# Leftover rows in the tiling of their neighbour, logits beside v, and a first tile over two queues

## The chip, the cores and the metric

One core of one Trainium2 chip. The metric is the device time of one execution in microseconds, the slowest (here the only) core. The kernel before takes 213.19 us (median of 3 runs, 213.16 to 213.43). The span in a profile is about 1.7 us shorter than the device time of the same run (211.4 against 213.11).

Engines are named as in the profile: PE is the matrix engine, PEld its weight loads, DVE VectorE, ACT ScalarE, POOL GpSimd, SP the queue engine that issues most DMAs.

## The reference

The input is x, 2048 x 512. It is layer-normalised, and two branches of it are added to x:

```
xn  = layernorm(x)
# A: 32 heads of 16, a dilated window of 8 keys (distance 0, 2, .. 14)
q, k, v = split(xn @ wqkv);  a = softmax(q.k over the window / 4);  A = (sum a v) @ wo
# B: gated MLP with spatial mixing, F = 1376, Fh = 688
z   = gelu(xn @ w_in);  z1 = z[:, :688];  z2 = layernorm(z[:, 688:])
g   = w_sp @ z2 + b_sp[:, None]           # w_sp is 2048 x 2048
B   = (z1 * g) @ w_out                    # w_out is 688 x 512
out = x + A + B
```

688 = 5 x 128 + 48: the last product contracts over five full chunks and 48 leftover rows. `g` for one tile of 128 rows is called a spatial product below; there are 16.

## The kernel before

All parts are cut. Tensors of 512 columns are handled in four blocks `tb` of 512 rows, each of four tiles; `o` counts output blocks of four tiles.

The matrix engine is used in several tilings. A full pass contracts over 128 rows into 128 columns. `wo` is applied in four row tiles of 32 (K=32, four passes into four PSUM banks run together), the leftover rows of `w_out` in two row tiles of 64 (K=48), logits and v in four column tiles of 32.

```python
def v_mm(d2):                                   # column tiling (0, 32*tb)
    for dd in range(2):
        for kc in range(C):
            for tb in range(TB):
                PE.matmul(pv[32*tb:32*tb+32, dd, :], wv[:, kc, 2*d2+dd, :], xnT[...],
                          ..., tile_position=(0, 32 * tb))
    A.copy(vp[:, 2*d2:2*d2+2, ...], pv[:])

def out_mm(o, last=False):
    for d in range(DH):                         # wo: row tiling, K=32, four at once
        for tb in range(TB):
            PE.matmul(pos[tb], op[32*tb:32*tb+32, d, ...], wo_r[32*tb:32*tb+32, d, :],
                      ..., tile_position=(32 * tb, 0))
    for h in range(2):
        pair = (2 * h, 2 * h + 1)
        for tb in pair:                         # leftovers: K=48, two at once
            r = slice(64 * (tb % 2), 64 * (tb % 2) + FH - FULL)
            PE.matmul(pos[tb], uT[r, o % 2, MCH-1, ...], wout[r, MCH-1, :],
                      ..., tile_position=(64 * (tb % 2), 0))
        for tb in pair:                         # five full passes each
            for m in range(MCH - 1):
                PE.matmul(pos[tb], uT[:, o % 2, m, ...], wout[:, m, :], ...)
        # ... add x, store
```

```python
load_x0(SP, 0); load_x0(A, 2); load_x0(SP, 1); load_x0(A, 3)   # four tiles of x, 128 KB each
load_wqk(SP, 0)                       # first half of the q and k weights, 512 KB
SP.dma_start(xall[:, 1], xblk[1])     # block 1 of x, 512 KB
load_wqk(SP, 1)                       # second half
# ... blocks 2 and 3 of x, then w_z2

warm_up(9)                            # nine passes on zeros, for PE's clock
# ... layer norm of tile 0, transposes, warm_up(2), tile 1, then the q and k products
```

```python
# order of the middle part (cut)
logits(3); prods(5); sm_max(0)
z2s(1, 1)
v_mm(0)
z2s(1, 2)
logits(4); ...
z2s(1, 3)
v_mm(1)
z2s(2, 0)
logits(5); ...
PE.transpose(pb[:], b16[:], ident[0:NT, 0:NT]);  A.copy(b_col[:], pb[:])   # b_sp to columns
...
z2_stat_act(2, 3)                     # 1/sqrt of z2's variance: root on ACT, reciprocal on DVE

for n in range(16):                   # one spatial product each
    z1_mm(n); gs = g_mm(n)
    # 2 to 5 DVE steps of softmax(..) * v ("applies")
    u_mul(n, gs)                      # z1 * g on DVE, then a DMA transpose into uT
    if n % 4 == 3 and o > 0: out_mm(o - 1); load_xr(o)
out_mm(3, last=True)
```

## Time and profile before

| what | value | view |
|---|---|---|
| span | 211.4 us | page |
| PE busy | 204.3 us, 97% | page, busy table |
| DVE, ACT busy | 83%, 45% | page, busy table |
| PE in one unbroken chain | from 24.2 to 207.8 us | chain of waits |
| PE idle that the list of waits finds, without its last line | 2.9 us | waits of PE |
| one output block | 8.74 us | chain in order of time |

The page's line of busy times, one engine after the other with its share of the span and its instructions:

```profile
PE 204.3 (97%) x1712; PEld 120.1 (57%) x1716; DVE 174.8 (83%) x248; ACT 95.2 (45%) x151; POOL 3.9 (2%) x20
```

The list of waits of PE in the kernel before (engine, line, whom it waited for; microseconds in total, times, the longest):

```profile
PE pwm L463 <- DVE r_qk L155: 1.3, 1, 1.3
PE pt L189 <- DVE r_x L182: 0.9, 1, 0.9
PE pq L265 <- ACT xnT L193: 0.7, 1, 0.7
PE po L424 <- issue: 0.5, 3, 0.2
```

All but the last lie before 8 us. A busy engine that waits for nobody can only be helped by giving it less to do, and the profile's busy time hides part of what there is to take away: while the engine changes its tiling it counts as busy. The chain in order of time (start, length, work) shows it. Each piece counts from the end of the piece before it to its own end, so the cost of a change falls on the group that comes behind it. First the round of logits (L305), one z group (L203), v (L339) and another z group in the kernel before:

```profile
45.99 0.98 PE pl L305 x16
46.96 1.27 PE pz L203 x8
48.24 1.89 PE pv L339 x32
50.12 1.27 PE pz L203 x8
51.39 0.98 PE pl L305 x16
```

A z group of eight passes alone takes 1.17 us (8 x 0.146); behind a column-tiled group it takes 1.27. Sixteen logits passes, four at a time, stream in 4 x 0.2155 = 0.862 us and take 0.98. The round takes 5.40 us. Second, an output block (L407 wo, L419 leftovers, L424 full passes; one matmul record is missing, which is the "issue" line):

```profile
158.23 3.56 PE po L407 x64
161.79 0.32 PE po L419 x2
162.12 0.16 issue
162.27 2.10 PE po L424 x9
164.38 0.32 PE po L419 x2
164.70 2.26 PE po L424 x10
166.97 1.17 PE pz L203 x8
```

A pair of leftovers streams in 0.2155 us and takes 0.32, and the ten full passes behind it take 2.26 for 2.16 streamed: around each pair the engine goes from one tiling to another and back.

### The profile page before, as it was taken

The numbers are of one execution on the slowest core, as the hardware profiler recorded it, in microseconds if no ns is written. First come the engines' busy times: TensorE is split into PE (matmuls) and PEld (weight loads), VectorE is DVE, ScalarE is ACT, GpSimd is POOL, SyncE is SP. The second block draws the span as 40 slices with busy tenths as digits, with TensorE's granted clock in tenths as the row PEclk, the third lists the DMA queues.
The fourth block names the chain that finished last, engine by engine and source line by source line (L and its number), as shares of the span: only waits on it lengthen the run. The fifth ranks groups of instructions, "written<-read, shape, count | busy, mean of one in ns | idle before, by whom it ended". The sixth has DMA issues, their size and how long they took to land.

```text
span 211.4 us, 4126 instructions
## 1 busy us (share of the span) xinstructions
PE 204.3 (97%) x1712; PEld 120.1 (57%) x1716; DVE 174.8 (83%) x248; ACT 95.2 (45%) x151; POOL 3.9 (2%) x20
## 2 busy tenths in 40 slices
PE   7799999999999999999999999999999999999993
PEld 2578544445565566666666664566664566664431
DVE  3988997969999996499999999899995688991413
ACT  2576797889987899931532120121211122221000
POOL 6000000000000000000000000000000000000000
PEclk9999999999999999999999999999999999999999
DMA  5973455000000979899456569998743241611143
GB/s 178 326 241 62 99 114 197 2 0 3 0 3 0 127 169 181 171 294 198 112 113 144 124 143 192 185 250 218 138 105 36 79 124 37 40 37 40 61 138 99
DMA packets 64705, 25.28 MB, mean 120 GB/s; under 512 B 53968, under 2 KB 64560, under 8 KB 64560
## 3 DMA queue, kind: packets, MB, share of 16 engines
q1 hardware_dynamic: 64256, 24.70, 53.2%
q10 hardware_dynamic: 432, 0.33, 0.5%
q8 instruction: 13, 0.21, 0.5%
q14 instruction: 4, 0.03, 0.0%
HBM read 10.03 MB, written 2.10 MB: 57 GB/s over the span
## 4 chain that ended last, share of the span: by engine, by line
PE 87%; DVE 8%; DMA 1%; ACT 1%; issue 1%; DVEq 0%
PE pg L374 35%; PE pz L203 18%; PE po L424 7%; PE pv L339 7%; PE pq L265 7%; PE po L407 7%; DVE stats L171 4%; PE pl L305 4%; DVE r_x L182 2%; DMA r_x<-in_A_x_dram 1%; DVE mv L172 1%; PE pa L424 1%; PE po L419 1%; ACT rstd L175 1%; ACT r_qk L270 0%
## 5 line engine op out<-in xcount | busy, mean ns | idle before, releaser
L374 PE MATMUL pg<-z,r_qk 128*128 128x344 bf16 x512 | 76.8, 309 | 0.0
L374 PEld LDWEIGHTS <-r_qk 128*128 128x128 bf16 x512 | 50.0, 98 | 24.9 <-issue 0.4
L203 PE MATMUL pz<-w_z,xnT 128*128 128x344 bf16 x256 | 41.7, 309 | 0.1
L377 ACT ACTIVATE gs<-pg,b_col 128x688 bf16<-128x688 f32 x16 | 13.3, 833 | 56.7 <-PE pg L374 56.7
L350 DVE TENSOR_TENSOR r_pr<-r_x,r_w 128x2048 bf16<-128x2048 bf16 x32 | 38.2, 1220 | 0.3
L354 DVE TENSOR_TENSOR r_pr<-r_pr 128x2048 bf16<-128x2048 bf16 x28 | 33.8, 1218 | 0.1
L203 PEld LDWEIGHTS <-xnT 128*128 128x128 bf16 x256 | 24.3, 98 | 16.2 <-issue 4.0
L265 PE MATMUL pq<-xnT,r_w 128*128 128x256 bf16 (+1 forms) x176 | 29.3, 321 | 0.7 <-ACT xnT L193 0.7
L298 DVE TENSOR_TENSOR r_pr<-r_qk 128x2048 bf16<-128x2048 bf16 x24 | 27.5, 1218 | 2.8 <-ACT r_qk L270 2.8
L265 PEld LDWEIGHTS <-r_w 128*128 128x128 bf16 x176 | 16.9, 98 | 11.3 <-issue 1.8
L412 DVE TENSOR_TENSOR r_qk<-po,r_qk 128x512 bf16<-128x512 f32 x14 | 9.0, 685 | 15.9 <-PE po L424 15.9
L257 ACT ACTIVATE z1u<-pz 128x688 bf16<-128x688 f32 x16 | 11.9, 744 | 22.4 <-PE pz L203 22.4
L270 ACT CAST r_qk<-pq 128x1024 bf16<-128x1024 f32 x16 | 15.8, 1012 | 5.4 <-PE pq L265 3.9
L424 PE MATMUL po<-r_w,uT 128*128 128x512 bf16 x66 | 15.6, 380 | 0.5 <-issue 0.5
L339 PE MATMUL pv<-xnT,r_w 128*32 128x512 bf16 x256 | 15.0, 383 | 0.0
L407 PE MATMUL po<-r_lg,r_pr 32*128 32x512 bf16 x224 | 14.5, 375 | 0.0
L171 DVE BATCH_NORM_STATS2 stats<-r_x 128x6 f32<-128x512 bf16 x16 | 10.7, 670 | 2.4 <-DMA r_x<-in_A_x_dram 2.4
L215 ACT ACTIVATE junk<-z 128x688 bf16<-128x688 bf16 x16 | 12.4, 778 | 0.5
L209 ACT ACTIVATE z<-pz 128x688 bf16<-128x688 f32 x16 | 11.9, 741 | 1.8 <-PE pz L203 1.6
L424 PEld LDWEIGHTS <-uT 128*128 128x128 bf16 x80 | 7.2, 98 | 9.4 <-issue 1.8
L339 PEld LDWEIGHTS <-r_w 128*32 128x32 bf16 x256 | 9.1, 140 | 4.7 <-issue 1.1
L407 PEld LDWEIGHTS <-r_pr 32*128 32x128 bf16 x256 | 6.2, 93 | 7.6 <-issue 1.0
(72 smaller groups left out, 132.4 us busy)
## 6 DMA issues: line engine op xcount, KB each, us to landing
r_lg<-in_A_wo_dram SPq DMA_DIRECT2D x4, 512.0 KB, 9.5
r_qk<-in_A_x_dram SPq DMA_DIRECT2D x16, 128.0 KB, 2.3
out_dram<-r_qk SPq DMA_DIRECT2D x15, 128.0 KB, 1.7
r_x<-in_A_x_dram SPq DMA_DIRECT2D x3, 512.0 KB, 7.3
w_z<-in_B_w_in_dram SPq DMA_DIRECT2D x2, 688.0 KB, 6.9
r_w<-in_A_wqkv_dram SPq DMA_DIRECT2D x4, 256.0 KB, 5.4
r_w<-in_B_w_out_dram SPq DMA_DIRECT2D x1, 640.0 KB, 5.1
r_w<-in_A_wqkv_dram SPq DMA_DIRECT2D x1, 512.0 KB, 4.2
```

Of the source, the lines that this page charges most:

```text
L171: V.bn_stats(stats[:, i, :], xall[:, j, tb, :])
L203: PE.matmul(pz[:, hh, 0:FHALF], xnT[:, kc, i * P:(i + 1) * P], wz[:, kc, hh * FHALF:(hh + 1) * FHALF], start=(kc == 0), stop=(kc == C - 1))
L265: PE.matmul(pq[:, s, b0 * P:b1 * P], wqk[:, kc, s * D + c * P:s * D + (c + 1) * P], xv[:, kc, b0:b1, j, :], start=(kc == 0), stop=(kc == C ...
L270: A.copy(dst[:, :, :, j, :], pq[:].rearrange("p s (b t) -> p s b t", b=TB))
L298: V.tensor_tensor(pr[g % 2][:, :, ww], q4, k4, ALU.mult)
L339: PE.matmul(pv[32 * tb:32 * tb + 32, dd, :], wv[:, kc, 2 * d2 + dd, :], xnT[:, kc, tb * TBS:(tb + 1) * TBS], start=(kc == 0), stop=(kc == ...
L350: V.tensor_tensor(pw_t[n], vp[:, :, off:off + P], a_sb[:, slot_w(w), ts].unsqueeze(1).broadcast_to([P, DH, P]), ALU.mult)
L354: V.tensor_tensor(pw_t[n] if dst is None else dst, pw_t[n], pw_t[m], ALU.add)
L374: PE.matmul(pg[:, hh, 0:FHALF], wsp[n % NWSP][:, k, :], z2[:, k, hh * FHALF:(hh + 1) * FHALF], start=(q == 0), stop=(q == NT - 1))
L377: A.activation(gs[:], pg[:, :, 0:FHALF], ACT.Identity, bias=b_col[:, i:i + 1])
L407: PE.matmul(pos[tb], op[32 * tb:32 * tb + 32, d, o * P:(o + 1) * P], wo_r[32 * tb:32 * tb + 32, d, :], start=(d == 0), stop=False, tile_po ...
L424: PE.matmul(pos[tb], uT[:, o % 2, m, tb * P:(tb + 1) * P], wout[:, m, :], start=False, stop=(m == MCH - 2))
```

## The change

The intent: fewer changes of tiling on PE, nothing on PE that a DMA can do, an earlier first tile, one ACT table load less.

1. The 48 leftover rows become two passes of K=24 in the 32-row tiling of `wo`, directly behind it. For that, z1 and the product u are written at an offset of 32 x (n mod 4) columns, so that the DMA transpose (now seven chunks) puts the leftovers of block `tb` at partitions 32 x tb.
2. v products 0 to 3 move next to the logits.
3. b_sp is transposed by the DMA and converted on POOL.
4. The second z2 root is computed on DVE with the integer estimate and three Newton steps that the first one used already; the softmax subtraction of the second half moves behind it.
5. x tiles 0 and 1 are loaded in halves over both queues.
6. Output blocks 0, 1, 2 come after products 8, 12 and 15 (before: 7, 11, 15), with the applies spread anew.

```diff
-MCH = 6
+MCH = 7
-FULL = (MCH - 1) * P
+FULL = (MCH - 2) * P
+KR = (FH - FULL) // 2
-APPLY_PER_G = [4, 4, 4, 4, 2, 2, 2, 2, 5, 5, 5, 5, 4, 4, 4, 4]
+APPLY_PER_G = [1, 2, 3, 4, 4, 4, 4, 4, 4, 6, 6, 6, 4, 4, 3, 1]
+OUT_AFTER = [8, 12, 15.5]
@@ loads at the start
-    load_x0(SP, 0)
+    load_x0(SP, 0, 0, 64)
+    load_x0(A, 0, 64, P)
+    load_x0(SP, 1, 0, 64)
+    load_x0(A, 1, 64, P)
     load_x0(A, 2)
-    load_x0(SP, 1)
     load_x0(A, 3)
@@ u_mul
+        z = 32 * (n % 4)
+        V.tensor_tensor(z1u[:, s, 0:FULL], g[:, 0:FULL], z1u[:, s, z:z + FULL], ALU.mult)
+        rest = z1u[:, s, FULL:FPAD].rearrange("p (a q) -> p a q", a=2)[:, :, z:z + KR]
+        V.tensor_tensor(rest, ...)
@@ out_mm, behind wo
+        for rt in range(2):
+            for tb in range(TB):
+                q, m = 32 * tb, MCH - 2 + rt
+                PE.matmul(pos[tb], uT[q:q + KR, o % 2, m, tb * P:(tb + 1) * P], wout[q:q + KR, m, :],
+                          start=False, stop=False, tile_position=(q, 0))
-            for tb in pair:
-                r = slice(64 * (tb % 2), 64 * (tb % 2) + FH - FULL)
-                PE.matmul(... tile_position=(64 * (tb % 2), 0))
@@ b_sp
-    SP.dma_start(b16[:], B_b_sp.rearrange("(j p) -> j p", p=P))
+    SP.dma_start_transpose(b16[:], B_b_sp.rearrange("(j p) -> j p", p=P))
+    G.tensor_copy(b_col[:], b16[:])
@@ middle part (the same for v 1, 2, 3)
     sm_max(0)
+    sm_sub(0)
+    v_mm(0)
     z2s(1, 1)
-    v_mm(0)
     z2s(1, 2)
@@
-    z2_stat_act(2, 3)
+    z2_stat_dve(2, 3)
+    sm_sub(1)
... (loads of w_out, loop over n with OUT_AFTER: cut)
```

More of the change, by code (lines that the diff above doesn't have):

```diff
@@ L113 @@
     warm = sb.tile([P, TBS], BF16, name="warm")
-    b16 = sb.tile([NT, P], BF16, name="b16")
+    b16 = sb.tile([P, NT], BF16, name="b16")
     b_col = sb.tile([P, NT], F32, name="b_col")
@@ L125, with load_x0 @@
     eps_t = sb.tile([P, 1], F32, name="eps_t")
-    def load_x0(E, tb):
-        E.dma_start(xall[:, 0, tb, :], x2[tb * TBS:tb * TBS + P, :])
+    def load_x0(E, tb, p0=0, p1=P):
+        E.dma_start(xall[p0:p1, 0, tb, :], x2[tb * TBS + p0:tb * TBS + p1, :])
     def load_wqk(E, h):
@@ L242, in z2_stat_dve @@
         z2_norms(j0, j1)
-    def z2_stat_act(j0, j1):
-        s = z2_var(j0, j1)
-        A.activation(zrstd[:, s], zvar[:, s], ACT.Sqrt, bias=eps_t[:])
-        V.reciprocal(zrstd[:, s], zrstd[:, s])
-        z2_norms(j0, j1)
     def z2_norm(i):
@@ L256, in z1_mm @@
         pz = zmm(i, w_z1)
-        A.activation(z1u[:, n % NZ1, 0:FH].rearrange("p (a b) -> p a b", a=2), pz[:, :, 0:FHALF],
+        z = 32 * (n % 4)
+        A.activation(z1u[:, n % NZ1, z:z + FH].rearrange("p (a b) -> p a b", a=2), pz[:, :, 0:FHALF],
                      ACT.Gelu_apprx_tanh)
@@ L319, in sm_max, with sm_sub @@
         V.tensor_tensor(m4[:, 0, :], m4[:, 0, :], m4[:, 1, :], ALU.max)
+    def sm_sub(hf):
+        l = lgf[:, :, 256 * hf:256 * hf + 256]
+        m4 = smt
         V.tensor_tensor(l, l, m4[:, 0, :].unsqueeze(1).broadcast_to([P, W, 256]), ALU.subtract)
@@ L382, in u_mul @@
         g = gs[:].rearrange("p a b -> p (a b)")
-        c0 = FULL if n % 2 else FH
-        V.tensor_tensor(z1u[:, s, 0:c0], g[:, 0:c0], z1u[:, s, 0:c0], ALU.mult)
-        if n % 2:
-            V.tensor_tensor(z1u[:, s, FULL + 64:FH + 64], g[:, FULL:FH], z1u[:, s, FULL:FH], ALU.mult)
+        z = 32 * (n % 4)
+        V.tensor_tensor(z1u[:, s, 0:FULL], g[:, 0:FULL], z1u[:, s, z:z + FULL], ALU.mult)
+        rest = z1u[:, s, FULL:FPAD].rearrange("p (a q) -> p a q", a=2)[:, :, z:z + KR]
+        V.tensor_tensor(rest, g[:, FULL:FH].rearrange("p (a q) -> p a q", a=2),
+                        z1u[:, s, z + FULL:z + FH].rearrange("p (a q) -> p a q", a=2), ALU.mult)
         SP.dma_start_transpose(uT[:, (n // 4) % 2, :, (n % 4) * P:(n % 4 + 1) * P], z1u[:, s, :])
@@ L416, in out_mm @@
             pair = (2 * h, 2 * h + 1)
-            for tb in pair:
-                r = slice(64 * (tb % 2), 64 * (tb % 2) + FH - FULL)
-                PE.matmul(pos[tb], uT[r, o % 2, MCH - 1, tb * P:(tb + 1) * P], wout[r, MCH - 1, :],
-                          start=False, stop=False, tile_position=(64 * (tb % 2), 0))
             alone = last and h == 1
             for tb in pair:
-                for m in range(MCH - 1):
+                for m in range(MCH - 2):
                     PE.matmul(pos[tb], uT[:, o % 2, m, tb * P:(tb + 1) * P], wout[:, m, :],
-                              start=False, stop=(m == MCH - 2))
+                              start=False, stop=(m == MCH - 3))
                 if alone and tb == 2:
@@ L562 @@
     G.memset(vp[0:32, :, 0:HALO], 0.0)
+    v_mm(1)
     z2s(1, 3)
-    v_mm(1)
     z2s(2, 0)
@@ L567 @@
     prods(7)
+    v_mm(2)
     z2s(2, 1)
-    v_mm(2)
     for n in range(4):
@@ L574 @@
     z2_stat_dve(0, 1)
+    v_mm(3)
     z2s(2, 3)
-    pb = ps_aux.tile([P, NT], BF16, name="pb", tag="aux")
-    PE.transpose(pb[:], b16[:], ident[0:NT, 0:NT])
-    A.copy(b_col[:], pb[:])
-    v_mm(3)
     z2s(3, 0)
@@ L597 @@
     sm_norm(1)
-    SP.dma_start(wout[:, 0:MCH - 1, :], B_w_out[0:(MCH - 1) * P, :].rearrange("(m p) n -> p m n", p=P))
-    for r in (0, 64):
-        SP.dma_start(wout[r:r + FH - FULL, MCH - 1, :], B_w_out[FULL:FH, :])
+    SP.dma_start(wout[:, 0:MCH - 2, :], B_w_out[0:FULL, :].rearrange("(m p) n -> p m n", p=P))
+    for tb in range(TB):
+        SP.dma_start(wout[32 * tb:32 * tb + KR, MCH - 2:MCH, :],
+                     B_w_out[FULL:FH, :].rearrange("(m r) n -> r m n", m=2))
     for tb in range(TB):
@@ L603, with outs @@
     load_xr(0)
+    def outs(at):
+        t = OUT_AFTER.index(at)
+        out_mm(t)
+        load_xr(t + 1)
     ap = [f for o in range(4) for f in apply_ops(o)]
@@ L610 @@
         gs = g_mm(n)
+        if n in OUT_AFTER:
+            outs(n)
         for _ in range(APPLY_PER_G[n]):
@@ L613 @@
         u_mul(n, gs)
+        if n + 0.5 in OUT_AFTER:
+            outs(n + 0.5)
         if n + NWSP < NT:
             load_wsp(n + NWSP)
-        if n % 4 == 3 and o > 0:
-            out_mm(o - 1)
-            load_xr(o)
     out_mm(3, last=True)
```

## The prediction

> **What bounds the kernel now.** The matrix engine. The page's busy table has PE at 97% of the 211.4 us span; the chain of waits is PE from 24.2 us to 207.8 us without a break; the list of waits finds 2.9 us of PE idle, nearly all before 8 us. Before 24 us the chain alternates DVE layer norm and PE and starts with tile 0 of x, which lands at 3.61 us (2.81 us after issue) and for which DVE waits 2.4 us. So only a shorter PE stream or an earlier first landing pays. DVE (83%) and ACT (45%) matter only if they begin to stall PE.
>
> **What changes in PE's stream.** The Trainium skill, "TensorEngine Tiling (Array Packing)", Key Properties, says that changing the tiling mode drains the array. The timeline agrees and gives the price, from start to start against the streaming rate (0.2155 us per 512 columns, 0.146 per 344):
>
> - Leftover rows of w_out. One output block takes 8.74 us: 16 row-tiled groups 3.56 (3.45 streamed), K=48 pair 0.32 (0.216 streamed), ten full passes 2.27 (2.16), pair 0.32, ten passes. Each of these four switches costs about 0.11 us. Afterwards two groups of four K=24 passes follow wo in its tiling: the streamed time is the same (2 x 0.2155), but one switch remains of four. Saving 0.33 us x 4 blocks = 1.3 us.
> - Logits beside v. Around each there is a switch in (0.10 us: the z group before takes 1.27 us instead of 1.17) and one out (logits 0.975 against 0.862; v 1.88 against 1.724). Four merges remove one of each: 4 x 0.21 = 0.85 us.
> - The transpose of b_sp leaves PE: 0.11 us.
> - x tile 0 by two queues: estimate 0.15 us; most of 2.8 us is fixed latency (a 64 KB store landed in 1.5 to 1.6 us, a 128 KB one in 1.7).
>
> Sum 2.4 us.
>
> **What moves and should cost nothing.** z2's root: DVE waited 1.84 us for ACT (table load 1.28, root 0.30), plus 0.20 reciprocal; twelve small operations about 0.2 us apart take 2.4 us instead. Their first result is needed 2.3 us after the spatial product starts; I expect 1.5 us of slack. ACT loses one table load. The seventh transpose chunk and the extra small multiply (8 x 0.1 us of DVE) are off the path. Later output blocks (after products 8, 12, 15) remove DVE idle (15.9 us waiting for them). Adding up DVE's operations (1.14 us per apply, 0.5 per product), I find it reaching the first output block 2.5 us before its first pair is done, the second 1.3 us before.
>
> **Prediction.** 213.19 - 2.4 = 210.8 us, range 209.9 to 211.9. Chances: faster by over 2% 0.05, within 2% 0.93, slower 0.02.
>
> **What would show it.** Output block 8.74 -> 8.41 us. The round of two z groups, logits and v 5.41 -> 5.2. No pb. First statistics at about 3.45 us instead of 3.64. Four instead of five ACT table loads. PE without stalls after 24 us. DVE's waits for output blocks well below 15.9 us.
>
> **What would make it wrong.** A stall of PE: at the first spatial product (z2 normalised too late), for PSUM after an output block (DVE or ACT behind), or at the early qk products, where PE already waited 0.17 us for the second half of wqk, so an earlier tile 0 may gain nothing. K=24 passes that don't run four at once would add 0.4 us or more per block. Slower DMA transposes could hold up the queue.

## More of the kernel before

At the start, the timeline of the SP queue (start, time to issue, what, how often) and of the first PE work:

```profile
0.80 0.90 SPq L129 DMA_DIRECT2D r_x<-in_A_x_dram  x2
1.74 0.99 SPq L136 DMA_DIRECT2D r_w<-in_A_wqkv_dram  x2
2.77 0.51 SPq L143 DMA_DIRECT2D r_x<-in_A_x_dram  x1
3.32 1.28 SPq L136 DMA_DIRECT2D r_w<-in_A_wqkv_dram  x2
```

```profile
5.89 0.40 PE L189 MATMUL pt<-ident,r_x 128*128 128x128 bf16 x4 [0.86 <-DVE r_x L182]
6.13 0.59 PE L463 MATMUL pwm<-warm 128*128 128x512 bf16 x2
```

The second half of wqk (the last SP line) is issued at 3.32 us, and the first transposes start at 5.89 us.

## The result and the profile after

The changed kernel takes 211.00 us in the median of six runs (210.63 to 211.89), the kernel before 213.17 us on the same chip. The ratio is 0.9906, 95% interval 0.9882 to 0.9931. Ratios here are the mean time of one kernel's fast runs over the mean of the other's in the same rounds, so not quite the ratio of the medians quoted. In a later round on another chip the same kernel took 210.75 us against 213.49 (ratio 0.9882, 0.9867 to 0.9897). The gain is 0.9 to 1.2%.

Busy times and the waits of PE after:

```profile
PE 202.7 (97%) x1727; PEld 121.3 (58%) x1731; DVE 176.9 (85%) x267; ACT 92.9 (44%) x148; POOL 5.7 (3%) x21
```

```profile
PE pwm L469 <- DVE r_qk L159: 1.3, 1, 1.3
PE pq L264 <- ACT xnT L197: 0.7, 1, 0.7
PE po L430 <- issue: 0.6, 4, 0.2
PE pt L193 <- DVE r_x L186: 0.6, 1, 0.6
```

PE still waits for nobody after its start. The round and the output block in the chain after (L304 logits, L342 v, L207 z, L411 wo, L417 leftovers, L430 full passes):

```profile
46.63 0.98 PE pl L304 x16
47.60 1.73 PE pv L342 x32
49.33 2.44 PE pz L207 x16
51.77 0.98 PE pl L304 x16
```

```profile
163.21 3.56 PE po L411 x64
166.78 0.43 PE po L417 x8
167.21 0.16 issue
167.37 4.26 PE po L430 x19
171.63 1.17 PE pz L207 x8
```

The round takes 5.14 us instead of 5.40. v takes 1.73 us, its streaming time (8 x 0.2155 = 1.724), and the two z groups pay for one change between them (2.44 = 2 x 1.17 + 0.10). The eight leftover passes take 0.43 us, exactly two groups of four in step, and the block takes 8.42 us instead of 8.74.

The start of this run did not get faster:

```profile
0.80 1.47 SPq L131 DMA_DIRECT2D r_x<-in_A_x_dram  x2
2.31 1.16 SPq L138 DMA_DIRECT2D r_w<-in_A_wqkv_dram  x2
3.51 0.51 SPq L147 DMA_DIRECT2D r_x<-in_A_x_dram  x1
4.06 1.05 SPq L138 DMA_DIRECT2D r_w<-in_A_wqkv_dram  x2
```

```profile
5.89 0.60 PE L193 MATMUL pt<-ident,r_x 128*128 128x128 bf16 x4 [0.62 <-DVE r_x L186]
6.29 1.06 PE L469 MATMUL pwm<-warm 128*128 128x512 bf16 x2
```

Three things are to be seen. SP needs 1.47 us to issue two halves where it needed 0.90 for two whole tiles, so the second half of wqk is issued 0.74 us later. The two warm-up passes take 1.06 us instead of 0.59: the array still runs at half its rate there, and everything behind on PE is 0.6 us late. (The record of the granted clock in the trace has full speed from 7.26 us in this run, from 4.66 us in the kernel before.) And the first transposes begin at 5.89 us as before, although the statistics of tile 0 began at 3.37 us instead of 3.64: DVE normalises tile 0 only after the statistics of tile 1, and these began at 4.42 us, against 4.46 before.

Since PE runs without a break, the span can be cut at three marks of the chain of waits: the start of the first logits, the start of the first spatial product, and the last addition on DVE. The last column is from there to the end of the span (the last store).

| kernel | first logits at | logits to first product | first product to last addition | end | span |
|---|---|---|---|---|---|
| before | 32.55 | 51.50 | 123.76 | 3.6 | 211.4 |
| after, first profile | 33.19 | 50.33 | 122.49 | 3.3 | 209.3 |
| after, second profile | 32.55 | 50.33 | 122.49 | 3.2 | 208.6 |

The two inner stretches lost 1.17 and 1.27 us, the same in both profiles of the changed kernel to 0.01 us. The start gained nothing in one profile and lost 0.64 us in the other. The last stretch is 0.3 to 0.4 us shorter after, though the change doesn't aim at it; experiments 1 to 4 have 3.4 to 3.6 us there, and the cause is open.

### The profile page after: what moved, and what is told of

Read it like the earlier page. It is cut to its first block, busy times and chain, and to the rows that moved or that the text cites. A ratio compares the mean times of both kernels' runs of the same rounds, so it can differ in the third digit from the quotient of the medians.

```text
span 209.3 us, 4186 instructions
## 1 busy us (share of the span) xinstructions
PE 202.7 (97%) x1727; PEld 121.3 (58%) x1731; DVE 176.9 (85%) x267; ACT 92.9 (44%) x148; POOL 5.7 (3%) x21
## 4 chain that ended last, share of the span: by engine, by line
PE 93%; DMA 3%; SPq 2%; issue 1%; DVE 0%; DVEq 0%
PE pg L377 36%; PE pz L207 18%; PE pq L264 12%; PE po L430 7%; PE po L411 7%; PE pv L342 7%; PE pl L304 4%; DMA r_w<-in_A_wqkv_dram 3%; PE pa L430 1%; PE po L417 1%; SPq L138 1%; SPq L131 1%; SPq L147 0%; PE pt L193 0%; DVE r_qk L422 0%
## 5 line engine op out<-in xcount | busy, mean ns | idle before, releaser
L207 PE MATMUL pz<-w_z,xnT 128*128 128x344 bf16 x256 | 40.9, 309 | 0.0
L207 PEld LDWEIGHTS <-xnT 128*128 128x128 bf16 x256 | 24.6, 98 | 14.7 <-issue 2.0
L422 DVE TENSOR_TENSOR r_qk<-po,r_qk 128x512 bf16<-128x512 f32 x14 | 9.0, 686 | 15.6 <-PE po L430 15.6
L430 PE MATMUL po<-r_w,uT 128*128 128x512 bf16 x66 | 14.9, 379 | 0.6 <-issue 0.6
L342 PE MATMUL pv<-xnT,r_w 128*32 128x512 bf16 x256 | 14.7, 380 | 0.0
L411 PE MATMUL po<-r_lg,r_pr 32*128 32x512 bf16 x224 | 14.5, 375 | 0.0
L430 PEld LDWEIGHTS <-uT 128*128 128x128 bf16 x80 | 7.5, 98 | 10.2 <-issue 1.7
L342 PEld LDWEIGHTS <-r_w 128*32 128x32 bf16 x256 | 9.5, 139 | 4.5 <-issue 0.3
L411 PEld LDWEIGHTS <-r_pr 32*128 32x128 bf16 x256 | 6.2, 93 | 7.7 <-issue 1.3
```

The lines of the kernel that those rows point to most:

```text
L207: PE.matmul(pz[:, hh, 0:FHALF], xnT[:, kc, i * P:(i + 1) * P], wz[:, kc, hh * FHALF:(hh + 1) * FHALF], start=(kc == 0), stop=(kc == C - 1))
L342: PE.matmul(pv[32 * tb:32 * tb + 32, dd, :], wv[:, kc, 2 * d2 + dd, :], xnT[:, kc, tb * TBS:(tb + 1) * TBS], start=(kc == 0), stop=(kc == ...
L411: PE.matmul(pos[tb], op[32 * tb:32 * tb + 32, d, o * P:(o + 1) * P], wo_r[32 * tb:32 * tb + 32, d, :], start=(d == 0), stop=False, tile_po ...
L430: PE.matmul(pos[tb], uT[:, o % 2, m, tb * P:(tb + 1) * P], wout[:, m, :], start=False, stop=(m == MCH - 3))
```

## The experiments

Twelve kernels were run, four at a time on one chip, with three to five timed rounds each beside the kernel before. All results were correct. Medians and ranges are of all runs unless one is named apart.

Two theories about the start stood against each other. Theory S: the split costs time at the start through what it does to the queues. Theory C: the lost 0.64 us is PE's clock waking late by chance.

### 1. The changed kernel with whole tiles of x

```diff
-    load_x0(SP, 0, 0, 64)
-    load_x0(A, 0, 64, P)
-    load_x0(SP, 1, 0, 64)
-    load_x0(A, 1, 64, P)
-    load_x0(A, 2)
+    load_x0(SP, 0)
+    load_x0(A, 2)
+    load_x0(SP, 1)
     load_x0(A, 3)
```

> The changed kernel with x tiles 0 to 3 loaded whole, as before. Theory S (the split of x tile 0 costs the head: longer queue issues push wqk's second half and the root's table load back, and PE starts qk 0.6 us later): mean time 0.3 to 0.8 us under the changed kernel's 211.0, that is 210.2 to 210.7, and first qk pass at about 7.85 us as before. Rival C (the 0.64 us loss in the head is the array clock waking late by chance, no matter how x is loaded): same mean and same spread as the changed kernel (210.6 to 211.9). Rival G (the split gains its 0.27 us of earlier first statistics): this one is 0.15 to 0.3 us slower, 211.2.

Measured: 210.78 us (210.33 to 211.16, and one run of 213.3), before 213.25; ratio 0.9891 (0.9851 to 0.9932). First logits at 32.69 us. The gain over the kernel before, 2.5 us, lies between the two measurements of the changed kernel (2.2 and 2.7 us, each against its own chip). So the split is worth nothing that these runs can resolve in the changed kernel. It doesn't cost 0.64 us either.

### 2. The kernel before with only the split

The edit is the reverse of the last one, applied to the kernel before.

> The kernel before with only the split of x tiles 0 and 1 over two queues. Theory S: 0.3 to 0.8 us slower than before (213.5 to 214.0), runs more spread than before's 0.4 us. Rival C: same mean as before within 0.2 us if before too has late-clock runs. Prediction's step (0.15 us gain): 213.0.

Measured: 213.67 us (213.19 to 214.77); ratio 1.0016 (0.9987 to 1.0044). That is the opposite sign of the predicted gain, with an interval that includes none. The profiled run was the slowest one, 214.77 us, and shows the wait that theory S speaks of at its longest. The first transposes start at 5.54 us, 0.35 us earlier than before, and then PE waits for the second half of wqk (timeline of PE):

```profile
9.45 0.39 PE L191 MATMUL pt<-ident,r_x 128*128 128x128 bf16 x4
11.69 0.61 PE L267 MATMUL pq<-xnT,r_w 128*128 128x256 bf16 x4 [1.85 <-DMA r_w<-in_A_wqkv_dram]
```

The DMA view of the first 14 us (GB/s in 40 equal slices of 0.35 us) shows how much has arrived by then. First the kernel before, then this one:

```profile
GB/s 0 0 0 0 0 111 190 375 369 341 225 233 298 209 307 325 331 328 306 285 268 303 291 326 345 367 363 347 344 342 354 354 345 353 355 369 363 381 338 192
```

```profile
GB/s 0 0 0 0 0 0 196 185 208 205 222 81 123 294 342 351 350 353 296 307 313 345 300 304 294 315 329 337 338 353 335 345 345 353 345 349 346 368 373 370
```

From 5 us on both move about 270 to 380 GB/s (the last slice before apart), near the highest rate that either reaches, so what is missing at 5 us is hardly made up. Until 4.55 us (13 slices) the kernel before has moved 750 KB and this one 430 KB (sum of the slices times 0.35 us). At 330 GB/s the missing 320 KB are about 1 us. The half tiles keep the issuing queues busy longer per byte (0.59 and 0.82 us for 64 KB each, against 0.40 and 0.43 for 128 KB), and all that comes behind the first tile is later. That the slower issue is the cause fits, but was not tried by itself. The split buys the first tile 0.3 us and delays the rest.

Bytes do not explain how long this wait is, though. Up to 10.5 us this run moved 225 GB/s in the mean and the second profile of the changed kernel (experiment 5) 226, against 251 in the kernel before. Yet the second half of wqk, issued at the same time, had landed at 10.72 us there and at 12.54 us here (chain of waits). What held it up in this run is open.

### 3. The kernel before with only the leftovers

The edit is point 1 of the change: the new `u_mul`, the leftovers in `out_mm`, the offset of z1 and the loads of `w_out`, with the output blocks at their old places.

> The kernel before with only the w_out leftovers as two K=24 passes in wo's tiling, old places of the output blocks. Theory (three tiling switches fewer per block): output block 8.42 us instead of 8.74, total 1.3 us faster, 211.9. Rival: at the old place, right after product 7, the leftovers of all four row tiles need the transposed product 3 before the first full pass, and PE would wait there: then less than 1.3 us.

Measured: 211.85 us (211.72 to 212.07), ratio 0.9926 (0.9902 to 0.9950). From first product to last addition 122.49 us instead of 123.76: 1.27 us, the whole of what the changed kernel gains in that stretch. The block in its chain is 3.56 + 0.43 + 4.42 us. PE doesn't wait, so the rival falls.

### 4. The kernel before with only the merges

```diff
     sm_max(0)
-    z2s(1, 1)
     v_mm(0)
+    z2s(1, 1)
     z2s(1, 2)
... (the same for v 1, 2, 3)
```

> The kernel before with only v products 0 to 3 moved next to the logits (b_sp still transposed on PE). Theory (one switch out and one in saved per merge, as the two traces show 5.40 to 5.14 us per round): 0.26 us x 4 = 1.05 us faster, 212.1. Rival: the gain of that stretch needs the emptier ACT (one table load less) too, then under 0.6 us with ACT-caused waits of PE.

Measured: 212.62 us (212.16 to 215.32), ratio 0.9986 (0.9941 to 1.0032). Two of the six runs spoil the ratio: one with a mean granted clock of 0.992 (214.13) and one of 215.32 at full clock whose cause I don't know. The other four lie at 212.16 to 212.71, 0.5 to 1.1 us under 213.25. The trace is clearer: from first logits to first product 50.54 us instead of 51.50, which is 0.96 us. The rival, that the gain needs the emptier ACT, falls. I had expected 1.05 us, four times 0.26. The chain shows why the fourth merge gives less: the transpose of b_sp (L578) still stands between the two z groups, and both take 1.27 us.

```profile
67.45 1.73 PE pv L339 x32
69.18 1.27 PE pz L203 x8
70.45 0.11 PE pb L578
70.56 1.27 PE pz L203 x8
```

In the changed kernel the two groups take 2.44 us together. The difference, 0.11 us of transpose and 0.10 of a change of tiling, is the 0.21 us between 50.54 and the changed kernel's 50.33. No run took the transpose out of the kernel before alone.

### 5 to 8. The changed kernel again, and three edits of it

> The changed kernel unchanged, for a common chip with the next three and to see how often its array clock wakes late. Expected 211.0 us median with full clock (0.996 or more), and single runs about 1.1 us above that where the mean clock is 0.990 to 0.992, as the kernel before has too (2 of 11 runs in the last round: 214.4).

Measured: 210.75 us (210.36 to 211.14, four runs), ratio 0.9882; all four runs have a mean granted clock of 0.998 or more. Its profile is the second one of the table above. Here the clock woke in time (the two warm-up passes take 0.59 us), the first transposes started at 5.71 us, 0.18 us earlier than in the kernel before, and PE gave that back further on (list of its waits):

```profile
PE pq L264 <- DMA r_w<-in_A_wqkv_dram: 0.3, 1, 0.3
```

Its first logits come at 32.55 us, exactly as before. So both theories hold a part: the 0.64 us of the first profile were the late clock (C), and the missing gain is the wait for wqk (S). The late clock isn't bound to the split: with whole tiles, the profile of experiment 4 has full speed from 6.69 us only.

All profiles together show where a head start of tile 0 goes. In the eight in which PE waits for no load after its first q and k pass, the first logits begin 24.64 to 24.66 us after that pass. It begins at 7.84 us in the kernel before. Three runs with a split tile had it clearly earlier: this one (7.65), experiment 2 (7.49) and experiment 11 (7.63). In these three PE then waits for wqk for longer than it had gained: 0.27, 2.1 and 0.5 us. In the others the gain was lost before that pass, to late statistics of tile 1 (first profile, experiments 7, 9 and 12, 4.42 to 4.52 us) or to a late clock (6 and 8, full speed from 6.90 and 6.58 us).

**Only tile 0 split**, tiles 1 and 3 whole on ACT's queue, tile 2 whole on SP's:

> The changed kernel, but only tile 0 split over the two queues; tile 1 and 3 whole on the scalar queue, tile 2 whole on the sync queue, so the sync queue issues two loads of x and the scalar queue three. Theory S (the split itself works, first transposes 0.35 us earlier as in the profile of before with only the split; it is the longer issue times on the sync queue, 0.74 us later for wqk's second half, that eat it): wqk's second half issued at about 3.4 us instead of 4.06, no wait of PE for it, full-clock runs 0.2 to 0.4 us under the changed kernel. Rival D (the head is bound by the bytes that must land before wqk's second half, 2 MB, whatever the issue order): same as the changed kernel or as with whole tiles, within 0.1 us.

Measured: 211.0 us (210.43 to 213.42), ratio 0.9905. No gain over the changed kernel in the same round (210.75), which fits rival D, though the runs scatter by more than the 0.1 us that D names, and the profiled run had a late clock. The second half of wqk was issued at 3.88 us, not at 3.4 as I expected: the issue of a whole tile next to another queue's half tile was as slow as that of a half (1.46 us for the two).

**The second half of wqk ahead of block 1 of x:**

```diff
-    SP.dma_start(xall[:, 1], xblk[1])
     load_wqk(SP, 1)
+    SP.dma_start(xall[:, 1], xblk[1])
```

> The changed kernel, but the second half of wqk is issued ahead of block 1 of x (512 KB each). Theory S and D both say PE's wait for wqk goes (it lands about 1.5 us earlier). Theory S: 0.2 to 0.4 us faster than the changed kernel. Rival: the wait only moves to block 1, whose statistics DVE wants at 9 to 10 us: then no gain, or slower, with DVE waiting for the load.

Measured: 212.47 us (212.30 to 213.83), ratio 0.9966, so 1.7 us slower than the changed kernel on the same chip. The wait for wqk is gone, and DVE waits for block 1 instead, in total, times and longest:

```profile
DVE stats L175 <- DMA r_x<-in_A_x_dram: 4.2, 3, 2.1
```

(2.1 of this is the first tile; the kernel before waits 2.4 us for it.) First logits at 34.56 us. Both loads are needed; here the order that brings one sooner brings the other later.

**The root back on ACT:**

```diff
-    z2_stat_dve(2, 3)
+    z2_stat_act(2, 3)
```

> The changed kernel, but z2's second root on ScalarE with its table load again. Prediction (costs nothing, off the path): same within 0.1 us, five table loads, PE without a wait at the first spatial product. Rival (with PE a microsecond earlier there, ACT's 1.6 us for table and root delays the v evictions until PE waits for PSUM or for normalised z2): 0.3 to 1 us slower, with a PE wait before the first spatial product or in it.

Measured: 210.57 us (210.41 to 210.82), ratio 0.9869. The inner stretches are 50.33 and 122.49 us, exactly those of the changed kernel, although DVE waits for ACT again:

```profile
DVE zrstd L251 <- ACT zrstd L250: 2.1, 1, 2.1
```

The move of the root is worth nothing in time. It saves ACT a table load of 1283 ns, and neither ACT nor DVE was what PE waited for. The Trainium skill, "ScalarE: Activation LUTs", What ACT_TABLE_LOAD costs, gives the same 1283 ns for the load; in this kernel it is simply off the path. The page adds a drain of about 1380 ns to each switch; the kernel before shows no such time, its root on ACT starts at 81.89 us, right behind the load that began at 80.59.

### 9. The changed kernel with the output blocks at their old places

```diff
-APPLY_PER_G = [1, 2, 3, 4, 4, 4, 4, 4, 4, 6, 6, 6, 4, 4, 3, 1]
-OUT_AFTER = [8, 12, 15.5]
+APPLY_PER_G = [4, 4, 4, 4, 2, 2, 2, 2, 5, 5, 5, 5, 4, 4, 4, 4]
... (the loop as before the change)
```

> The changed kernel with the output blocks and the apply counts at their old places (after products 7, 11, 15). Prediction (the move is worth nothing in itself; PE streams either way): same within 0.1 us, 210.75 with full clock, no PE wait after 24 us. Rival (the leftovers of all four row tiles now come before the full passes, so at the old place PE waits for the transposed product 3 or for PSUM): 0.3 us or more slower, with such a wait in the list.

Measured: 210.58 us (210.48 to 210.71), ratio 0.9856 (0.9781 to 0.9930, wide because of one run of the kernel before at 215.94). The stretch takes 122.49 us in both. The move is worth nothing, and nothing waits at the old places.

### 10 to 12. Two attempts at the start

Block 1 of x in two halves around the second half of wqk:

```diff
-    SP.dma_start(xall[:, 1], xblk[1])
+    SP.dma_start(xall[:, 1, 0:2], xblk[1][:, 0:2])
     load_wqk(SP, 1)
+    SP.dma_start(xall[:, 1, 2:4], xblk[1][:, 2:4])
```

> The changed kernel, but block 1 of x is loaded as tiles 0 and 1 ahead of wqk's second half and tiles 2 and 3 behind it. Theory D (head bound by the bytes ahead of what PE needs next): 256 KB fewer bytes ahead of wqk's second half, at some 0.33 MB/us about 0.75 us earlier, so PE's 0.27 us wait for it goes and the earlier first tile comes through: 0.2 to 0.4 us faster, 210.4 with full clock. Rival: tiles 2 and 3 then come late for their statistics at 11 to 13 us and the gain is gone, as with the whole block behind (1.7 us slower).

Measured: the three timed runs took 210.74, 210.80 and 210.93 us, the same as the changed kernel in the round before (210.36 to 211.14); the expected 0.2 to 0.4 us didn't come. The profiled run took 753.27 us. All of PE ran at about a quarter of its speed in it (a spatial product's 32 passes took 17.59 us instead of 4.67), so its trace says nothing about the edit.

Twelve warm-up passes instead of nine:

```diff
-    warm_up(9)
+    warm_up(12)
```

> The changed kernel with 12 warm-up passes instead of 9, so that PE has no gap between the warm-up (ends about 5.2 us) and the first transposes (5.7 us). Theory C (the rare runs at mean clock 0.990 to 0.992, 1.1 us slow, and the profiles in which the warm-up passes at 6 us still run at 0.43 us apart, are the array clock waking late because the activity has a gap): no run below 0.995 and a median 0.1 to 0.3 us lower. Rival: chance of another kind, the late runs stay; and where the clock is still slow at 5.2 us the three extra passes (0.43 us each) delay the first transposes by up to 0.7 us.

Measured: 210.53 us (210.24 to 211.03, four runs), ratio 0.9856 (0.9792 to 0.9920); no run has a mean clock under 0.997. The changed kernel had none in its own four runs of the round before either, so this doesn't show that the longer warm-up changes anything.

Both edits:

> Both of the last two edits together, as a candidate for a better version: if both theories hold 210.2 with full clock and no late run; if one falls, the sum of what each did alone.

Measured: 210.30 us (210.24 to 211.06), ratio 0.9851 (0.9787 to 0.9915). It is the lowest median of all, and its profile has no wait for wqk, but first logits come at 32.58 us, no earlier than in the changed kernel. With four runs each it can't be told from 9 and 11. I don't call it a better version. Nor does it show what the wait for wqk costs: the statistics of tile 1 began at 4.45 us in it, so the first transposes have no head start (5.89 us in the kernel before). The kernel before, without a head start, had no such wait either.

```profile
5.93 0.39 PE L194 MATMUL pt<-ident,r_x 128*128 128x128 bf16 x4
```

Whether the start gets faster when tile 1 and the second half of wqk both come in time stays untried; experiment 10 was meant to show it and lost its profile.

### Scatter

Runs with a mean granted clock of 0.990 to 0.992 were 0.6 to 1.6 us slower than the full-clock median of their kernel, in the kernel before (214.37 and 214.40 among 11 runs) as in the changed one (211.89 and 211.85 among 6). None of these runs has a trace, so what was slow in them isn't shown. The mean clock doesn't count a late wake-up: the profiled run of experiment 4, with full speed from 6.69 us only, has a mean of 1.000. The Trainium skill, "TensorE: Matmul & The Clock Gate", Part 1, says that PE's clock is released by a busy window that runs freely and isn't tied to the start of a kernel, so the wake-up moves from run to run. The traces agree: full speed begins between 4.09 us (experiment 2) and 7.26 us (first profile of the changed kernel), and the same warm-up passes at 6 us took 1.06 us in that profile and 0.59 in the other. A few runs at full clock were some 2.5 to 3 us slow (213.3, 213.42 and 215.32 of edited kernels, 215.94, 216.03 and 216.29 of the kernel before); their cause stays open.

## Why the prediction was right or wrong

Predicted 210.8 us, measured 211.00 and 210.75.

- **What bounds the kernel**: right. PE has no break after the start in either kernel, and edits that only touched DVE, ACT or the place of the output blocks (8 and 9) left both inner stretches the same to 0.01 us.
- **Leftovers, 1.3 us**: right. The block went from 8.74 to 8.42 us, 1.27 us in the stretch, and alone (3) it gave the same. The K=24 passes do run four at once.
- **Merges, 0.85 us**: right, a little too small: 0.96 us alone in the trace. I took the saving as one entry and one exit; the traces show 0.05 us more in three of the four merges (the fourth, beside b_sp's transpose, gave 0.16 us in 4), since v next to the logits also lost its own start-up (1.73 against 1.89 us in the chain).
- **b_sp, 0.11 us**: the stretch shows 0.21 us that the merges alone don't have, predicted 0.11: beside the transpose its change of tiling went too, which I had not counted. The chain of 4 shows both, but b_sp had no run of its own.
- **Tile 0 over two queues, 0.15 us**: wrong. First statistics came at 3.37 us (3.31 in the second profile) instead of 3.64, earlier than I said. But the step "earlier first tile, earlier stream" failed: alone the split came out 0.4 us slower in the median (2, not resolved by the interval), in the changed kernel it is worth nothing (1). I had named the reason as a risk, the second half of wqk, but took the issue of half tiles for free. They take as long as or longer than whole ones. By 4.55 us 320 KB less had arrived (2), and where the first q and k pass came up to 0.35 us earlier, PE waited 0.27 to 2.1 us for wqk (2, 5, 11). I also left out that DVE takes the statistics of tile 1 first, which came too late to pass the gain on in four profiles. The Trainium skill, "Trainium Kernel Development and Optimization", Key Constraints, says that queues of different engines run on the same 16 DMA engines and that issuing from several "only saves the sequencer's issue time". These runs agree with the first half: the highest slice of the first 14 us is 381 GB/s before and 383 in the second profile after. The second half isn't tested here, since the kernel before issues from two queues already. The split only made six issues of four, and slower ones (1.47 against 0.90 us for two on SP).
- **Root, table loads**: right in time (8). Four table loads instead of five, as said. The slack was larger than the 1.5 us I gave: the first normalised tile was ready at 82.6 us and needed at about 85.9 (its pair of passes is the ninth of the first product: 83.52 + 16 x 0.146 us).
- **DVE's waits "well below 15.9 us"**: wrong. They are 15.6 us. I added up the first two blocks (2.67 and 0.60 us before the first pairs, 2.5 and 1.3 predicted) and left out the last two, whose waits of 4.8 and 5.0 us come at the end, when DVE has nothing left to do. Off the path, it cost nothing.

The sum worked: 1.27 + 0.96 + 0.21 = 2.44 us against 2.4, with 0 in place of 0.15 for the start. The two large terms were right by their mechanism. That the total fits so closely is in part luck: the merges and b_sp gave 0.21 us more than forecast, which makes up for the start. Why the first round gave 211.00 and the second 210.75 isn't shown; the late clock of the first profile (0.64 us) and two of the six timed runs, 1 us slow for a reason not shown, fit it.

## What to carry to other kernels

When the matrix engine is never idle, look for changes of its tiling: a short group between two groups of another tiling costs 0.2 us or more beyond its streaming time, all of it counted as busy, so put work of one tiling together, even if the passes become smaller and more. Before you split a first load over two queues, see whether the time before the first stall is bound by one transfer's latency or by the bytes that must all land; in the second case the split only changes which one is late. See also what the engine takes next: the head start of tile 0 had to pass the statistics of tile 1. Judge single parts of a microsecond by stretches of the trace between two marks, since those repeat to 0.01 us where whole times scatter by 1 us.

## What the Trainium skill lacked or had wrong

- "TensorEngine Tiling (Array Packing)", Key Properties, says that a change of tiling mode drains the array, but gives no price. Here each change costs 0.10 to 0.16 us in the chain, and the profile counts it as busy. Two column-tiled groups with different weights behind one another (logits, then v) pay none between them (1.73 us for v in the chain, streamed 1.724).
- "TensorE: Matmul & The Clock Gate", Part 1, mentions the clock stuck at a quarter for over 50 us. One execution here ran at about a quarter for its whole 751.5 us, and its mean granted clock is given as 1.0, because the trace holds no record of the clock at all. The page calls the clock's trace events unreliable; that a run's recorded mean clock can miss such a state altogether isn't on it.
- No page that I read says that half tiles issued at the same time from two queues take longer to issue than whole tiles: 0.59 and 0.82 us for 64 KB on SP, against 0.40 and 0.43 us for 128 KB; and in the experiment with only tile 0 split, a whole tile behind a half one on SP was slow as well. Why is open.
